# Sink scores in column tiles, an earlier weight row and a new order of loads in a windowed-attention and SwiGLU kernel

## The chip, the cores and the metric

The kernel runs on one core of a Trainium2 chip. Its time is the device time of one execution, in microseconds (us). The page and the trace come from one execution under the hardware profiler; its span runs from the first to the last instruction. The engines are called PE (TensorE), DVE (VectorE), ACT (ScalarE), POOL (GpSimd) and SP (SyncE). SP, ACT and POOL can also issue transfers, each on its own queue.

## The reference

Attention with a few sink keys and a sliding window, followed by a gated feed-forward network. There are 4 batches, 8 heads, 768 positions and a head size of 64; `n_sink` is 4 and `window` is 128.

```
scores = q @ k.T / sqrt(64)
keep   = (key < 4) or (0 <= query - key < 128)
a      = softmax(scores where keep)
x      = (a @ v), heads side by side: 3072 tokens x 512
xn     = x / sqrt(mean(x*x) + 1e-6) * rms_g
out    = (silu(xn @ w_gate) * (xn @ w_val)) @ w_out     # 512 -> 1536 -> 512
```

All inputs and the output are fp32; the kernel computes in bf16 with fp32 sums.

## The kernel before

**Blocks.** The 3072 tokens are 24 blocks `g` of 128 tokens, six in a batch `b` (`t` is the place in the batch). A query sees the keys of its own block and of the block before, so for each key block the kernel computes the scores of two query blocks at once (`nq = 2`; one in the last block of a batch). A query block that starts at position 256 or later (`t >= 2`) has its sink keys outside these two blocks, and they are handled apart.

**Steps of one block.** Loads of q, k and v go through the POOL queue, which casts fp32 to bf16. For the first blocks, a few loads (`F32_LOADS`) go through SP in fp32 and are cast by ACT or DVE (`cast`, L318). Blocks below `QK_DMA_FROM = 8` have q and k transposed on PE (`pe_t`, L415) and copied out of PSUM (`copy_t`, L422); the later ones are transposed by a DMA that SP issues (`dma_t`). Then come:
- `mask_bias` (L437), for blocks below `PE_MASKS`: a matmul of 512 columns writes -32768 where the mask forbids, into each of the four score banks, and the scores add to it.
- `scores` (L455): 8 matmuls of 64 rows, in pairs of row tiles. A block in `SPLIT` has its two query blocks scored apart.
- `exps` (L468) on ACT.
- For blocks that have no bias matmul: a mask that multiplies the exponentials on DVE (`mask_dve`, L485), or, from `POOL_MASK_FROM` on and for `t > 0`, selects on POOL (`mask_pool`, L490 and L495).
- `av` (L504, L514, L519) on PE, `normal` (L530, L531) and `rms` (L546 to L563) on DVE, `square` (L539) on ACT. `rms` multiplies by `gb`, the RMS weight row on all 128 partitions.
- The result x is transposed on PE (`pe_x`, L578) and copied (`copy_x`, L584), or, from block `X_DMA_FROM` on, by a DMA from SP (`dma_x`, L590).

**The weight row.** `grow` is one row of 512 fp32 numbers. `unit_gb` (L398) multiplies it with a column of ones on PE, which spreads it over the partitions, and `scale_gb` (L401) copies it out on ACT.

**Sinks.** `sink_k` (L594 to L598) puts the four sink keys of each head into a tile `ksk` that is zero elsewhere. `sink_s` (L621) computes the sink scores of two or four query blocks: four matmuls, one for each pair of heads, all adding into the same 128 rows of one PSUM bank; each has the 128 columns of `ksk` that begin at its pair's place, in which only that pair's 8 rows are not zero. `sink_e` (L629) takes the exponential, `sel` and `headm` bring the sink values of v into the matching rows (`sink_v`, L603; `sink_vm`, L612), and `av` adds one matmul with both.

**Feed-forward.** Four blocks make a group `G`. For each group the gate and value matmuls (L755) fill tiles of 128 x 512, cut into 4, 2 or 1 token chunks (`CHUNKS`). ACT takes tanh (L762), DVE makes `p` (L768) and `hT` (L778). `project` (L788) multiplies with `w_out`, ACT evacuates (L796) and SP stores.

**Order.** The order on every engine is worked out when the program is built, by the class `Plan`: each step has an estimated duration, its needs, a priority (smaller goes first) and the PSUM banks that it takes. The planner always places next the step that can start first, by its own clock; on a tie the smaller priority wins. Its model of transfers is `land`. The result is a fixed order: at run time each engine works in it and waits where data is missing. `LOADS` gives the order of loads on the POOL queue, `gate_of` holds a block's scores back until a given feed-forward step (`GATE_LEAD` steps earlier than its place), and `warm` puts up to `WARM` matmuls on zeros where PE would be idle.

Of the kernel before, what the change touches and what calls it, by code (L numbers as in the profile page):

```python
# [10 lines left out]
ACT = mybir.ActivationFunctionType  # L11
FP32 = mybir.dt.float32
BF16 = mybir.dt.bfloat16
I32 = mybir.dt.int32

P = 128
# [10 lines left out]
class Plan:  # L27
# [21 lines left out]
    def land(self, ring, first, work):  # L49


        r = self.rings
        if ring == "POOL":
            begin = max(first, r["POOL"], r["HW"])
            r["POOL"] = begin + (1.4 * work if begin < 8500 else work)
            self.loads -= 1
            return r["POOL"] + 520
        if ring == "HW":
            r["HW"] = max(first, r["HW"]) + work
            return r["HW"] + 900  # L60
        begin = max(first, r["TR"], r["POOL"])
        if self.loads:
            r["POOL"] = max(r["POOL"], first) + work
            work *= 2
        r["TR"] = begin + work
        return r["TR"] + (350 if ring == "TR" else 650)

    def run(self):
        free, users = dict(self.START), {}
        self.loads = sum(o["ring"] == "POOL" for o in self.ops)  # L70
        wait = {o["at"]: set(o["needs"]) for o in self.ops}
        cand = {e: [] for e in free}
        left = len(self.ops)
        for o in self.ops:
            for t in o["needs"]:
                users.setdefault(t, []).append(o)
            if not o["needs"]:
                for e in o["ways"]:
                    cand[e].append(o)
        busy, warm, mode, order = [], False, 0, []  # L80
        while left:
            first = None
            for e, found in cand.items():
                for o in found:
                    k = len(o["takes"])
                    if k > len(self.banks):
                        continue
                    ready = o["ready"] + self.HOP[e] if o["ready"] else 0
                    if k:
                        ready = max(ready, sorted(self.banks.values())[k - 1] + 40)  # L90
                    start = max(free[e], ready)
                    key = (start, o["prio"], ready, o["at"])
                    if first is None or key < first[0]:
                        first = key, e, o
            if first is None:
                raise RuntimeError("stuck: %s" % [
                    (o["gives"], list(wait[o["at"]])) for o in self.ops if o["at"] in wait
                ][:20])
            (start, *_), e, o = first
            for x in o["ways"]:  # L100
                cand[x].remove(o)
            wait.pop(o["at"])
            left -= 1
            ns, lat, fn = o["ways"][e]
            if e == "PE":
                busy = [(a, d) for a, d in busy if a > start - 3413]
                warm = start - free[e] < 4000 and (warm or sum(d for a, d in busy) > 3000)
                ns = ns if warm else 2 * ns
                if o["mode"] != mode:
                    ns, mode = ns + 110, o["mode"]  # L110
                busy.append((start, ns if mode < 2 else 0))
                lat = ns + 180
            for s in o["takes"]:
                i = min(self.banks, key=lambda i: (self.banks[i], i))
                del self.banks[i]
                self.held[s] = i
            free[e] = start + ns
            end = start + lat
            if o["ring"] is not None:
                end = self.land(o["ring"], end, o["work"]) + self.LATE  # L120
            for s in o["drops"]:
                self.banks[self.held[s]] = end + 12
            for t in o["gives"]:
                for x in users.pop(t, ()):
                    x["ready"] = max(x["ready"], end + 12)
                    w = wait[x["at"]]
                    w.discard(t)
                    if not w:
                        for way in x["ways"]:
                            cand[way].append(x)  # L130
            order.append((start, end, e, fn, o))
        return order
# [3 lines left out]
def kernel(  # L136
# [13 lines left out]
    nc = tc.nc  # L150

    B, H, S, D = q.shape
# [12 lines left out]
    GN = GB * P  # L165
    VW = D + 1
    HW = 4 * VW
    KSW = P + 2 * NS
    inv_sqrt_d = 1.0 / math.sqrt(D)
    F32_LOADS = ("qs0","ks0","qs1")  # L170
    GROW = "ACT"
    CAST_DVE = 1500
    MASKS_PRIO = -5
    POOL_AT = (0,1)
    DEPTH = 8
    LOADS = "k-1 v-0 qkv-2 w-0-2 v-1 qkv-3 w-2-4 w-4-6 w-6-8 w-8-9 w-9-12 qkv-4 wo-0-6 qkv-5 wo-6-12 qkv-8 qkv-6 qkv-7"
    LOADS += "".join(f" qkv-{g}" for g in range(9, NB))
    PE_MASKS = 4
    POOL_MASK_FROM = 14
    X_DMA_FROM = 8  # L180
    QK_DMA_FROM = 8
    LD = 16
    GATE_FROM = 6
    LOAD_LEAD = 9
    LEAD_FROM = 9
    WARM = 20
    GATE_LEAD = 10
    T_LEAD = 3
    SPLIT = (0,1,2)
    CHUNKS = (4,2,2)  # L190
    GB_PRIO = 2000

# [59 lines left out]
        dve(60, lambda b=b: nc.vector.memset(V16[b][:, :, :, D:VW], 1.0),  # L252
            gives=[("vone", b)], prio=-97 + b if b == 0 else -50)
    dve(150, lambda: nc.vector.memset(ones, 1.0), gives=["ones"], prio=-96)
    dve(70, lambda: nc.vector.memset(sel, 0.0), gives=["sel0"], prio=-39)
    if WARM:
        zeros = const.tile([P, P], BF16, name="zeros")
        dve(70, lambda: nc.vector.memset(zeros, 0.0), gives=["zeros"], prio=-99.6)
# [29 lines left out]

    def make_sel():
        nc.vector.tensor_copy(  # L290
            out=sel[:, 0:H * NS].rearrange("p (h s) -> p h s", s=NS),
            in_=ident[:, 0:NS].unsqueeze(1).to_broadcast((P, H, NS)),
        )
        nc.vector.reduce_sum(
            out=headm, in_=ident[:, 0:H * NS].rearrange("p (h s) -> p h s", s=NS),
            axis=mybir.AxisListType.X,
        )

# [2 lines left out]
    dve(130, other_bias, [("bias", 0)], [("bias", 1)], -60)  # L301
    dve(220, cut_ident, ["ident"], ["idnos"], -59)
    dve(700, make_masks, [("bias", 0), ("bias", 1)], ["masks"], MASKS_PRIO)
    dve(300, make_sel, ["ident", "sel0"], ["sel", "headm"], MASKS_PRIO + 1)

# [92 lines left out]
    def scale_gb():  # L400
        nc.scalar.mul(gb, BANK.pop(("gb",)), C3)  # L401

    pe(864, unit_gb, ["ones", "grow", ("s", 0, 0)], ["gbm"], GB_PRIO, takes=[("gb",)], mode=2)
    act(490, scale_gb, ["gbm", "table"], ["gb"], drops=[("gb",)])

    def qk_tile(b):
# [183 lines left out]
        nc.sync.dma_start_transpose(out=x_out(g), in_=T.pop(("xr", g)))  # L590

    def sink_k(b):
        ks = T["ksk", b] = sink.tile([P, HP * KSW], BF16, name="ksk")
        nc.vector.memset(ks, 0.0)  # L594
        ksv = ks.rearrange("p (h c) -> p h c", c=KSW)
        for hi in range(2):
            pr = slice(hi * D, (hi + 1) * D)
            nc.vector.tensor_copy(  # L598
                out=ksv[pr, :, hi * NS:(hi + 1) * NS], in_=T["qkT", b][pr, 1, :, 0:NS],
            )  # L600
# [17 lines left out]
    def sink_s(b, t, n):  # L618
        ps = bank(("ss", b, t))
        for hp in range(HP):  # L620
            nc.tensor.matmul(  # L621
                out=ps[:, 0:n * P], lhsT=T["ksk", b][:, hp * P:(hp + 1) * P],
                rhs=T["qkT", b][:, 0, hp, t * P:(t + n) * P],
                start=(hp == 0), stop=(hp == HP - 1),
            )

    def sink_e(b, t, n):
# [17 lines left out]
    for g in range(NB):  # L645
# [84 lines left out]
        if t == 0:  # L730
            dve(600, lambda b=b: sink_k(b),
                [("kT", g), ("s", g + 1)] + ([("ss", b - 2, i) for i in ((2, 4) if b - 2 < 2 else (2,))]
                               if b >= 2 else []), [("ksk", b)], 0.1 * g)
            for half in range(2):
                pe(115, lambda b=b, half=half: sink_v(b, half), [("v", g), ("vone", b), "sel", ("s", g)],
                   [("vs", b, half)], pa + 14, takes=[("vs", b, half)])
                dve(340, lambda b=b, half=half: sink_vm(b, half), [("vs", b, half), "headm"]
                    + ([("av", NT * (b - 2) + NT - 1, u) for u in range(2)] if b >= 2 else [])
                    + ([("vsk", b, 0)] if half else []),
                    [("vsk", b, half)], 0.1 * g, drops=[("vs", b, half)])  # L740
            for t0, n in ((2, 2), (4, 2)) if b < 2 else ((2, 4),):
                pe(4 * (n * 53 + 3), lambda b=b, t0=t0, n=n: sink_s(b, t0, n),
                   [("ksk", b), ("s", g + 1)] + [("qT", g + t0 + i) for i in range(n)],
                   [("ss", b, t0)], -1000.0 + 10 * (g + t0) + 2, takes=[("ss", b, t0)])
                act(n * 107 + 55, lambda b=b, t0=t0, n=n: sink_e(b, t0, n),
                    [("ss", b, t0), "table"] + ([("av", g - 1, u) for u in range(2)] if b else []),
                    [("esk", b, t0 + i) for i in range(n)], early, drops=[("ss", b, t0)])
# [169 lines left out]
```

The softmax here doesn't subtract the row's maximum and nothing guards it: scores larger than these inputs give would overflow.

## Time and profile before

| what | value |
|---|---|
| time, median of 3 runs | 249.78 us (248.58 to 250.07) |
| profiled run, its span | 249.03 us, 247.3 us |
| granted PE clock, mean of the span | 0.999 |
| DVE busy 60 to 66, 66 to 91, 91 to 103 us | 5.6 of 6, 24.1 of 25, 11.2 of 12 us |
| DVE busy 103 to 115, 115 to 132, 132 to 152 us | 11.1 of 12, 8.9 of 17, 18.8 of 20 us |
| first feed-forward matmul (L755) | 20.79 us |
| first matmul of feed-forward group 3 | 142.44 us |
| DMA queue of POOL, share of 16 engines | 76.3% |

Part 1 of the page gives the busy time of each engine. PE and PEld are matmuls and loads of their stationary operand. A group row reads: line, engine, operation, out<-in, shapes and count, then busy us and mean ns, then the idle time before it and what ended it. The chain of waits, in order of time, gives start and length in us of each piece that the end can be traced back through. DMA digits in the page are at 8 or 9 tenths for the first half of the span.

### The profile page before, as it was taken

What the parts mean: (1) busy time and instruction counts of PE and PEld (TensorE: products, weight loads), DVE (VectorE), ACT (ScalarE), POOL (GpSimd) and SP (SyncE); (2) the same over time, 40 slices, a digit from 0 to 9 for tenths busy, and PEclk for the clock granted to TensorE, in tenths of its full rate; (3) what the DMA queues carried; (4) which work ended last, traced back from release to release, by engine and by line L of the source; (5) the groups of instructions that cost most, each with busy time, mean ns of one, the idle gap of its engine ahead of it and who ended that gap; (6) DMA issues with size and microseconds to landing.
All of it is one profiled execution on the core that took longest, in us unless ns stands there. A gap on an engine that the chain in (4) does not pass through costs nothing.

```text
span 247.3 us, 5553 instructions
## 1 busy us (share of the span) xinstructions
PE 239.0 (97%) x2122; PEld 151.1 (61%) x2122; DVE 181.0 (73%) x477; ACT 129.5 (52%) x278; POOL 91.8 (37%) x121
## 2 busy tenths in 40 slices
PE   5899999999999999999999999999999999999994
PEld 2467998875788875587786544445555444444443
DVE  4278878798999999997377999998369980277700
ACT  3578366869655926662537466273556421333211
POOL 8976655759424756733703201230331000000000
PEclk9999999999999999999999999999999999999999
DMA  8999999999999999999990362201231002200022
GB/s 133 175 174 195 190 188 188 157 113 148 180 197 126 156 137 155 167 209 145 155 149 19 100 157 42 48 19 55 77 106 25 11 11 85 85 3 0 0 85 85
DMA packets 112523, 27.48 MB, mean 111 GB/s; under 512 B 102641, under 2 KB 109553, under 8 KB 112498
## 3 DMA queue, kind: packets, MB, share of 16 engines
q0 software_dynamic: 79664, 13.77, 76.3%
q1 hardware_dynamic: 32688, 13.25, 30.1%
q8 instruction: 16, 0.26, 0.4%
q10 hardware_dynamic: 146, 0.13, 0.2%
q14 instruction: 9, 0.07, 0.1%
HBM read 28.31 MB, written 6.29 MB: 140 GB/s over the span
## 4 chain that ended last, share of the span: by engine, by line
PE 84%; DVE 9%; DMA 3%; issue 2%; ACT 1%; POOLq 0%
PE v L755 23%; PE g L755 23%; PE o L788 22%; PE s L455 4%; DMA k<-in_k_dram 3%; PE av L519 2%; PE av L514 2%; PE ss L621 2%; DVE x L531 2%; DVE r L559 2%; DVE hT L778 1%; PE av L504 1%; PE o_last L806 1%; DVE p L768 1%; DVE xr L563 1%
## 5 line engine op out<-in xcount | busy, mean ns | idle before, releaser
L755 PE MATMUL v<-xnt,wv 128*128 128x128 bf16 (+2 forms) x528 | 70.9, 282 | 0.3 <-DVE hT L778 0.2
L762 ACT ACTIVATE th<-g 128x512 bf16<-128x512 f32 x72 | 43.0, 600 | 51.3 <-PE g L755 48.4
L755 PE MATMUL g<-xnt,wg 128*128 128x128 bf16 (+2 forms) x528 | 69.6, 282 | 0.2 <-DVE hT L778 0.2
L768 DVE SCALAR_TENSOR_TENSOR p<-th,g 128x512 bf16<-128x512 bf16 x72 | 48.4, 683 | 27.4 <-ACT th L762 27.2
L788 PE MATMUL o<-wo,hT 128*128 128x512 bf16 x276 | 65.3, 379 | 0.0
L755 PEld LDWEIGHTS <-wg 128*128 128x128 bf16 x528 | 43.6, 98 | 19.3 <-issue 0.3
L468 ACT ACTIVATE e<-s 128x512 bf16<-128x512 f32 (+1 forms) x108 | 49.2, 526 | 11.6 <-PE s L455 10.2
L755 PEld LDWEIGHTS <-wv 128*128 128x128 bf16 x528 | 43.2, 98 | 19.7 <-issue 1.2
L778 DVE TENSOR_TENSOR hT<-p,v 128x512 bf16<-128x512 bf16 x72 | 47.1, 681 | 2.9 <-PE v L755 2.2
L788 PEld LDWEIGHTS <-hT 128*128 128x128 bf16 x276 | 25.2, 98 | 27.0 <-issue 1.7
L490 POOL TENSOR_SCALAR_AFFINE_SELECT e<-e 128x512 bf16<-128x512 bf16 x18 | 11.6, 650 | 53.1 <-ACT e L468 42.8
L326 POOL DMA_DIRECT2D v<-in_v_dram x24 | 21.3, 889 | 14.7 <-DMA q<-in_q_dram 9.8
L322 POOL DMA_DIRECT2D k<-in_k_dram x23 | 20.4, 889 | 15.4 <-DMA v<-in_v_dram 8.5
L796 ACT ACTIVATE osb<-o 128x512 f32<-128x512 f32 x23 | 13.8, 601 | 19.5 <-PE o L788 19.5
L322 POOL DMA_DIRECT2D q<-in_q_dram x22 | 19.5, 886 | 11.1 <-DMA k<-in_k_dram 5.0
L539 ACT ACTIVATE sq<-x 128x512 bf16<-128x512 bf16 x24 | 15.2, 632 | 14.9 <-DVE x L531 14.8
L531 DVE TENSOR_TENSOR x<-av,rden 128x256 bf16<-128x256 f32 x48 | 20.4, 424 | 1.7
L563 DVE SCALAR_TENSOR_TENSOR xr<-x,r,gb 128x512 bf16<-128x512 bf16 x24 | 18.4, 765 | 0.9
L519 PE MATMUL av<-v,e 128*128 128x65 bf16 x192 | 17.0, 195 | 0.0
L514 PE MATMUL av<-v,e 128*128 128x65 bf16 x160 | 14.7, 193 | 0.2 <-ACT e L468 0.2
L455 PE MATMUL s<-qkT 64*128 64x256 bf16 (+1 forms) x216 | 14.9, 258 | 0.1
L485 DVE TENSOR_TENSOR e<-e,masks 128x1024 bf16<-128x1024 bf16 (+1 forms) x22 | 13.6, 635 | 1.4 <-ACT e L468 1.4
(72 smaller groups left out, 182.3 us busy)
## 6 DMA issues: line engine op xcount, KB each, us to landing
out_dram<-osb SPq DMA_DIRECT2D x23, 256.0 KB, 2.4
v<-in_v_dram POOLq DMA_DIRECT2D x24, 128.0 KB, 10.0
k<-in_k_dram POOLq DMA_DIRECT2D x23, 128.0 KB, 10.7
q<-in_q_dram POOLq DMA_DIRECT2D x22, 128.0 KB, 11.3
wo<-in_moe_w_out_dram POOLq DMA_DIRECT2D x2, 768.0 KB, 12.3
wg<-in_moe_w_gate_dram POOLq DMA_DIRECT2D x4, 256.0 KB, 8.0
wv<-in_moe_w_val_dram POOLq DMA_DIRECT2D x4, 256.0 KB, 8.3
stage<-in_q_dram SPq DMA_DIRECT2D x2, 256.0 KB, 4.7
```

Of the source, the lines that this page charges most:

```text
L322: nc.gpsimd.dma_start(out=T[name, g], in_=block_of(src, g))
L326: nc.gpsimd.dma_start(out=V16[b][:, t, :, 0:D], in_=block_of(v, g))
L455: nc.tensor.matmul(out=BANK[slot][:, j * 256 + n0 * P:j * 256 + n1 * P], lhsT=qkT[pr, 1, hp, t * P:(t + 1) * P], rhs=qkT[pr, 0, hp, (t + n ...
L468: nc.scalar.activation(out=T["e", g, u][:, 2 * hi:2 * hi + 2, n0:n1, :].rearrange("p x n c -> p x (n c)"), in_=ps.rearrange("p (j c) -> p ...
L519: nc.tensor.matmul(out=dest, lhsT=T["e", g, u][:, x, 0, :], rhs=V16[b][:, t, h, :], start=(t == 0), stop=True, skip_group_check=True,)
L531: nc.vector.tensor_tensor(out=T["x16", g][:, 4 * u:4 * u + 4, :], in0=pvv[:, :, 0:D], in1=rden.unsqueeze(2).to_broadcast((P, 4, D)), op=AL ...
L563: nc.vector.scalar_tensor_tensor(out=T["xr", g], in0=T.pop(("x16", g)).rearrange("p h d -> p (h d)"), scalar=r[:, 3:4], in1=gb, op0=ALU.mu ...
L755: nc.tensor.matmul(out=ps[:, i * n:(i + 1) * n], lhsT=w_sb[:, kt, ft * P:(ft + 1) * P], rhs=T["xnt", G][:, kt, cols], start=(kt == 0), sto ...
L762: nc.scalar.activation(out=T["th", key], in_=BANK[("g", key)], func=ACT.Tanh, scale=0.5,)
L768: nc.vector.scalar_tensor_tensor(out=T["p1", key], in0=T.pop(("th", key)), scalar=1.0, in1=BANK.pop(("g", key)), op0=ALU.add, op1=ALU.mult,)
L778: nc.vector.tensor_tensor(out=T[hk][:, i:i + n, cols], in0=T.pop(("p1", key)).rearrange("p (n c) -> p n c", n=n), in1=BANK.pop(("v", key)) ...
L788: nc.tensor.matmul(out=BANK[("o", G, tb)], lhsT=T["h", G, ft // 4][:, ft % 4, tb * P:(tb + 1) * P], rhs=wo[:, ft, :], start=(ft == 0), sto ...
```

## The change

1. **Sink scores.** The four matmuls of `sink_s` write four different sets of 32 PSUM rows (`tile_position=(0, hp * 32)`), each from 32 columns of a smaller `ksk`, instead of adding into one set of 128. `sel` and `headm` are laid out to match, and the memset of `sel` goes.
2. **Weight row.** `grow` is loaded by SP instead of ACT (`GROW`), and `unit_gb` no longer needs the first scores of block 0.
3. **Loads.** `F32_LOADS` are k and q of block 0, in that order; q of block 1 goes to the head of `LOADS`. The first weights and v of block 1 pass block 2's q, k and v; near the end blocks 8 and 6 change places.
4. **Where work is done.** `PE_MASKS` 4 to 2, `POOL_MASK_FROM` 14 to 16, `X_DMA_FROM` 8 to 9, `POOL_AT` (0,1) to (1,2) (the two selects that build the identity and the bias, among the loads on POOL), `CAST_DVE` 1500 to 600.
5. **Planner.** `WARM` 20 to 30, `GATE_LEAD` 10 to 6, `LEAD_FROM` 9 to 10, `SPLIT` without block 2; the model of an fp32 load that begins late, and of the modes that count as PE activity, changes.

```diff
-            r["HW"] = max(first, r["HW"]) + work
+            begin = max(first, r["HW"])
+            r["HW"] = begin + (1.25 * work if begin > 2500 else work)
...
-                busy.append((start, ns if mode < 2 else 0))
+                busy.append((start, ns if mode != 2 else 0))
...
-    KSW = P + 2 * NS
+    SW = P // HP
-    F32_LOADS = ("qs0","ks0","qs1")
-    GROW = "ACT"
-    CAST_DVE = 1500
+    F32_LOADS = ("ks0","qs0")
+    GROW = "SP"
+    CAST_DVE = 600
-    POOL_AT = (0,1)
+    POOL_AT = (1,2)
-    LOADS = "k-1 v-0 qkv-2 w-0-2 v-1 qkv-3 w-2-4 ... qkv-5 wo-6-12 qkv-8 qkv-6 qkv-7"
+    LOADS = "q-1 k-1 v-0 w-0-2 v-1 qkv-2 qkv-3 w-2-4 ... qkv-5 wo-6-12 qkv-6 qkv-8 qkv-7"
-    PE_MASKS = 4
-    POOL_MASK_FROM = 14
-    X_DMA_FROM = 8
+    PE_MASKS = 2
+    POOL_MASK_FROM = 16
+    X_DMA_FROM = 9
-    LEAD_FROM = 9
-    WARM = 20
-    GATE_LEAD = 10
+    LEAD_FROM = 10
+    WARM = 30
+    GATE_LEAD = 6
-    SPLIT = (0,1,2)
+    SPLIT = (0,1)
...
-    pe(864, unit_gb, ["ones", "grow", ("s", 0, 0)], ["gbm"], GB_PRIO, takes=[("gb",)], mode=2)
+    pe(1000, unit_gb, ["ones", "grow"], ["gbm"], GB_PRIO, takes=[("gb",)], mode=2)
...
-        ks = T["ksk", b] = sink.tile([P, HP * KSW], BF16, name="ksk")
+        ks = T["ksk", b] = sink.tile([P, HP * SW], BF16, name="ksk")
...
-                out=ps[:, 0:n * P], lhsT=T["ksk", b][:, hp * P:(hp + 1) * P],
+                out=ps[hp * SW:(hp + 1) * SW, 0:n * P],
+                lhsT=T["ksk", b][:, hp * SW:(hp + 1) * SW],
                 rhs=T["qkT", b][:, 0, hp, t * P:(t + n) * P],
-                start=(hp == 0), stop=(hp == HP - 1),
+                start=True, stop=True, tile_position=(0, hp * SW), skip_group_check=True,
...
-                pe(4 * (n * 53 + 3), lambda b=b, t0=t0, n=n: sink_s(b, t0, n),
+                pe(n * 53 + 16, lambda b=b, t0=t0, n=n: sink_s(b, t0, n),
...
-                   [("ss", b, t0)], -1000.0 + 10 * (g + t0) + 2, takes=[("ss", b, t0)])
+                   [("ss", b, t0)], -1000.0 + 10 * (g + t0) + 2, takes=[("ss", b, t0)], mode=3)
```

More of the change, by code (lines that the diff above doesn't have):

```diff
@@ L167 @@
     HW = 4 * VW
-    KSW = P + 2 * NS
+    SW = P // HP
     inv_sqrt_d = 1.0 / math.sqrt(D)
-    F32_LOADS = ("qs0","ks0","qs1")
-    GROW = "ACT"
-    CAST_DVE = 1500
+    F32_LOADS = ("ks0","qs0")
+    GROW = "SP"
+    CAST_DVE = 600
     MASKS_PRIO = -5
-    POOL_AT = (0,1)
+    POOL_AT = (1,2)
     DEPTH = 8
-    LOADS = "k-1 v-0 qkv-2 w-0-2 v-1 qkv-3 w-2-4 w-4-6 w-6-8 w-8-9 w-9-12 qkv-4 wo-0-6 qkv-5 wo-6-12 qkv-8 qkv-6 qkv-7"
+    LOADS = "q-1 k-1 v-0 w-0-2 v-1 qkv-2 qkv-3 w-2-4 w-4-6 w-6-8 w-8-9 w-9-12 qkv-4 wo-0-6 qkv-5 wo-6-12 qkv-6 qkv-8 qkv-7"
     LOADS += "".join(f" qkv-{g}" for g in range(9, NB))
-    PE_MASKS = 4
-    POOL_MASK_FROM = 14
-    X_DMA_FROM = 8
+    PE_MASKS = 2
+    POOL_MASK_FROM = 16
+    X_DMA_FROM = 9
     QK_DMA_FROM = 8
@@ L254 @@
     dve(150, lambda: nc.vector.memset(ones, 1.0), gives=["ones"], prio=-96)
-    dve(70, lambda: nc.vector.memset(sel, 0.0), gives=["sel0"], prio=-39)
     if WARM:
@@ L290, in make_sel @@
         nc.vector.tensor_copy(
-            out=sel[:, 0:H * NS].rearrange("p (h s) -> p h s", s=NS),
-            in_=ident[:, 0:NS].unsqueeze(1).to_broadcast((P, H, NS)),
+            out=sel.rearrange("p (a s) -> p a s", s=NS),
+            in_=ident[:, 0:NS].unsqueeze(1).to_broadcast((P, P // NS, NS)),
         )
         nc.vector.reduce_sum(
-            out=headm, in_=ident[:, 0:H * NS].rearrange("p (h s) -> p h s", s=NS),
+            out=headm.rearrange("p (x i) -> p x i", i=2),
+            in_=ident.rearrange("p (x i s) -> p x i s", x=HP, s=NS)[:, :, 0:2, :],
             axis=mybir.AxisListType.X,
@@ L303 @@
     dve(700, make_masks, [("bias", 0), ("bias", 1)], ["masks"], MASKS_PRIO)
-    dve(300, make_sel, ["ident", "sel0"], ["sel", "headm"], MASKS_PRIO + 1)
+    dve(300, make_sel, ["ident"], ["sel", "headm"], MASKS_PRIO + 1)
     def block_of(src, g):
@@ L592, in sink_k @@
     def sink_k(b):
-        ks = T["ksk", b] = sink.tile([P, HP * KSW], BF16, name="ksk")
+        ks = T["ksk", b] = sink.tile([P, HP * SW], BF16, name="ksk")
         nc.vector.memset(ks, 0.0)
-        ksv = ks.rearrange("p (h c) -> p h c", c=KSW)
+        ksv = ks.rearrange("p (h c) -> p h c", c=SW)
         for hi in range(2):
```

## The prediction, made before the change was run

> **What bounds the kernel now.** I read the page's busy shares first, then the waits of TensorE (PE) after the start, then the chain that ended last, then the groups by shape.
>
> The page's first part:
>
> ```profile
> PE 239.0 (97%) x2122; PEld 151.1 (61%) x2122; DVE 181.0 (73%) x477; ACT 129.5 (52%) x278; POOL 91.8 (37%) x121
> ```
>
> A busy PE is not proof of a bound, since matmul records overlap. The waits of PE alone between 20 and 244 us are the proof:
>
> ```profile
> PE ss L621 <- DVE qkT L422: 0.3, 1, 0.3
> PE v L755 <- DVE hT L778: 0.2, 1, 0.2
> PE g L755 <- DVE hT L778: 0.2, 1, 0.2
> ```
>
> After 20 us PE lacks work for 0.7 us in total. So the span is the time until PE is fed without gaps (about 20.5 us) plus a dense stream, and only two things move it: an earlier dense stream, or less in the stream (or a new hole in it). The start is a different stage; the chain in order of time (start, us, what):
>
> ```profile
> 1.32 6.58 DMA k<-in_k_dram
> 7.94 0.61 PE k L415 x4
> ...
> 8.76 0.54 PE s L455 x8
> ...
> 9.95 2.00 PE gb L398 x2
> 11.95 0.54 PE s L455 x8
> 12.49 0.56 PE av L519 x8
> ...
> 13.80 0.43 PE q L415 x4
> 14.23 0.43 PE k L415 x4
> ...
> 17.47 0.33 PE x L578 x4
> ```
>
> The fp32 spread of the weight row (gb) sits between the first and second scores, for 2.00 us, and everything below queues behind it. Four transposes take 0.43 us at 14.23 and 0.33 at 17.47: PE is at half clock until about 14.7 us. The groups by shape (busy us, mean ns):
>
> ```profile
> L437 PE MATMUL s<-bias,ident 128*128 128x512 bf16 x12 | 3.1, 382 | 0.0
> L621 PE MATMUL ss<-qkT,ksk 128*128 128x256 bf16 x16 | 2.4, 273 | 0.3 <-DVE qkT L422 0.3
> L621 PE MATMUL ss<-qkT,ksk 128*128 128x512 bf16 x8 | 2.1, 379 | 0.0
> L485 DVE TENSOR_TENSOR e<-e,masks 128x1024 bf16<-128x1024 bf16 x18 | 12.1, 684 | 1.4 <-ACT e L468 1.4
> ```
>
> These means hold latency that the next matmul hides; the chain gives the pace: four matmuls of 512 columns take 0.86 us, four of 256 take 0.43 to 0.44, four transposes 0.23 in a dense stretch.
>
> **What the Trainium skill says.** (1) "TensorEngine Tiling (Array Packing)", Key Properties: tiles run independently, but changing the tiling mode drains the array. Before has one change of mode to compare: after eight 64-row score matmuls the next matmul starts about 0.1 us late (129.97 start, 0.43 us of streaming in pairs, next at 130.52). (2) "TensorE: Matmul & The Clock Gate", Measured speedup vs the span model: three column tiles gave 2.38 times, not 3. No run here shows column tiles yet. (3) The tiling page, Restrictions: column tiles lose the fast weight load; with 24 weight loads of 32 columns I put that at nothing. (4) The clock page: PE idles at half clock and is released by activity; the trace agrees, with its four bias matmuls of 583 to 631 ns at 3.9 us and 379 to 420 ns from 14.7 us on.
>
> **The change, part by part.**
>
> *Sink scores.* Six groups of four matmuls: four groups of 256 columns, two of 512. In the stream they cost 4 x 0.43 + 2 x 0.86 = 3.4 us; the first (19.93) lies in the start, so 3.0 us lie in the dense stream. If four tiles give about 3 times (estimate from the clock page's 2.38 for three), 1.0 us is left. Each group brings one or two changes of mode at about 0.1 us: 5 x 0.14 = 0.7. Net -1.3 us. Bounds: -1.8 (perfect overlap, one change each), +0.9 (no overlap at all, two changes). The smaller ksk (memset of 272 words, 285 ns, becomes 64 words) frees under 0.2 us of DVE, four times: off the path.
>
> *Bias matmuls of blocks 2 and 3.* Eight matmuls leave, 0.86 us each block. Block 3's set (22.71 us) is in the dense stream: -0.9. Block 2's (16.61) is in the start and counted there. In return DVE multiplies four tiles more, 4 x 684 ns = 2.7 us. Block 2's lie near 20 us, block 3's near 37 us, where DVE is busy 6.7 of 10 and 21.2 of 25 us; PE waited for DVE only 0.7 us in all, so 0. Bounds 0 to +0.7 (one mask of latency on a hidden tile's chain).
>
> *Weight row.* grow's issue goes from ACT (0.53 us) to SP, between the two fp32 loads; qs0 is then issued at about 1.85, where the second load stood at 1.33, so its landing (5.7) slips to about 6.2. gb no longer waits for the first scores, so its 2.0 us at half clock come before them. PE has idle time there (4.0 of the first 10 us, in the table of stretches), but make_bias now stands behind the second load on the POOL queue (POOL_AT), 0.9 us later, so bias matmuls start at about 4.75 instead of 3.87. PE needs, at half clock, 1.86 (bias) + 2.0 (gb) + 4 x 0.43 to 0.63 (transposes) before both scores of block 0: first scores at 9.2 to 10 instead of 8.76, second at 9.8 to 10.6 instead of 11.95. Net -1.3 to -2.1 on the chain to av and x.
>
> *Loads.* q of block 1 goes from the SP queue (fp32, 256 KB) to the head of the POOL queue. Behind it on that queue wait all others, one issue (0.89 us) later each; w-0-2 and v-1 pass qkv-2. In the order of landing, the first feed-forward tile needs w-2-4: it landed at 18.8 (wg) and 20.2 (wv), used at 20.79 and 23.58. One HWDGE load less (third landing 2.4 us after the second, with k-1 in between) against one software load more (0.85 us each at steady pace): w-2-4 the same or up to 0.6 earlier. So PE can't be dense before about 18.5: the start gains at most 2.3 us. I take -1.6 (with block 2's bias matmuls gone from it); bounds -0.5 to -2.3.
>
> *Later weights.* wg of columns 6 to 8 landed at 24.18 and is used at 26.80; wg 9 to 12 at 28.94, used at 31.3; k-4 at 32.6, used at 35.7. That is 2.3 to 3 us of room, just enough for a PE that is 1.6 + 0.9 us ahead.
>
> *Other moves.* Block 8's x is transposed on PE (+0.23 us, and a copy of 0.42 on DVE or 0.6 on ACT) and leaves SP's queue (issue 1.19 us, 6.8 us to landing): +0.3, and the DMA transposes behind it come a little earlier. Masks of blocks 14 and 15 go from POOL (8 of 32 selects, 0.64 us each) to DVE, 4 x 684 ns; DVE is busy only 8.9 of 17 us from 115 to 132: 0. WARM fillers, ten more of 0.107 us at half clock, lie in gaps of the start; SPLIT loses block 2 and costs its second scores a wait for q-3 (landed 16.0, used at 19): 0.
>
> Sum: -1.6 - 0.9 - 1.3 + 0.3 = -3.5 us of the 247.3 us span: 243.8. The profiled run took 249.03, the other runs shown 248.58 to 250.07; -1.4% of the median is **246.3 us**.
>
> **The rivals.**
>
> *Half gain.* The start stays bound by weights and by half-clock PE (-0.5), or the column tiles do not overlap (+0.9 for -1.3). For it: the room before w-2-4 is thin, and no trace shows the overlap. The first alone gives -2.4 us (247.4), the second -1.3 (248.5), both -0.2 (249.6).
>
> *Slower: feed-forward group 3 starves.* Its first matmul starts at 142.44, and the last x it needs lands at 141.8 (DVE row xr at 139 us and its DMA transpose): 0.6 us of room. GATE_LEAD 6 instead of 10 makes block 15's scores wait for the seventh tile of group 2 (end at 122.2) where they ran at 118.06: 4.1 us. If blocks 14 and 15 carry this to their x, PE has used up group 2's projections and stands still: +4.1 less the last sink's 0.5, span 250.9, time 253.4. Against it: block 15's tiles lie ready from 123 us on and are used only after 131, so 8 us of delay are needed before this decides, and a PE that is 3 us ahead uses up 3 of them.
>
> *All the gain there is.* Start at -2.3 and sinks at -1.8 give -4.7 us, 245.0. More fillers may also release the clock before 14.7 us; for: PE has more to do early; against: the weights at 18.5 us cap what the start can give. Below 244.5 something is needed that I don't see.
>
> **How the numbers follow.** A run-to-run spread of 0.6% makes about 1% the least that can be told from no change. My forecast, from all its gain to the edge of half gain (244.5 to 247.2), 0.52; better than that 0.10; half gain (247.3 to 250.2) 0.25; starved, above 250.2, 0.13. Faster by over 1% (below 247.3): 0.63; slower by over 1% (above 252.3): 0.10; between: 0.27. The range 243.8 to 250.6 leaves out about 0.07 below and 0.12 above.
>
> **What would show it.** gb ahead of the first scores, and second scores at 10 to 11 us; first g tile at 18.5 to 19.3; L437 with 8 matmuls; each 512-column sink group ending under 0.5 us from its start to the next matmul; PE's waits after 20 us still under 1.5 us; group 3's first g at about 139. The forecast is wrong if sink matmuls start 0.2 us apart, if the first g tile stays at 20.5 or later, or if PE waits several us for hT, xnt or a weight load.

## The result, and the profile after

The changed kernel takes 246.64 us (median of four runs, 245.98 to 246.97), the kernel before 249.75 us (four runs, 248.58 to 250.07). The ratio is 0.9881, with a 95% interval of 0.9841 to 0.992: 1.2% faster, where 246.3 us was forecast. The span of the profiled run went from 247.3 to 244.3 us. Line numbers are one to two higher in the changed kernel: scores L456, bias matmuls L438, weight row L399, sinks L622, feed-forward L757.

First the busy shares of the page, and then the waits of PE between 20 and 241 us (what PE waited for: us in total, times, longest).

```profile
PE 232.6 (95%) x2098; PEld 147.8 (61%) x2120; DVE 183.7 (75%) x482; ACT 131.2 (54%) x276; POOL 88.8 (36%) x114
```

```profile
PE o L790 <- issue: 0.6, 4, 0.2
PE g L757 <- DVE rden L531: 0.3, 1, 0.3
PE g L757 <- DMA wg<-in_moe_w_gate_dram: 0.2, 1, 0.2
```

PE is still the bound: 1.1 us of waits after 20 us (0.7 before). Busy PE fell by 6.4 us, but not all of that is gain: 22 matmul records are missing in this trace (2098 against 2120 weight loads), and a matmul's record holds latency (a second run of the changed kernel, with all 2120 records, has 235.9 us busy). The groups by shape:

```profile
L486 DVE TENSOR_TENSOR e<-e,masks 128x1024 bf16<-128x1024 bf16 x26 | 17.5, 686 | 0.9 <-ACT e L469 0.8
...
L622 PE MATMUL ss<-qkT,ksk 128*32 128x256 bf16 x16 | 1.2, 283 | 0.0
L399 PE MATMUL gb<-grow,ones 1*128 1x512 f32 x2 | 1.1, 640 | 0.0
L438 PE MATMUL s<-bias,ident 128*128 128x512 bf16 x4 | 1.0, 378 | 0.0
L622 PE MATMUL ss<-qkT,ksk 128*32 128x512 bf16 x8 | 0.8, 390 | 0.0
```

Eight bias matmuls with `ident` are gone, DVE has eight more masks of 686 ns, and the sink groups are busy for 2.0 us in place of 4.5. A mean of 390 ns for one 512-column sink matmul looks unchanged (379 before); only the timeline shows that four now run together. The timeline of PE (start, length, what) before, and then after:

```profile
165.04 1.03 PE L621 MATMUL ss<-qkT,ksk 128*128 128x512 bf16 x4
165.91 1.03 PE L755 MATMUL v<-xnt,wv 128*128 128x512 bf16 x4
```

```profile
171.62 0.40 PE L622 MATMUL ss<-qkT,ksk 128*32 128x512 bf16 x4
171.96 0.61 PE L456 MATMUL s<-qkT 64*128 64x256 bf16 x8
```

From the first sink matmul to the next other matmul: 0.87 us before, 0.34 us after. A group of 256 columns took 0.44 and takes 0.22 us.

The start of the profiled run, PE alone (a bracket is idle time and what ended it):

```profile
8.46 0.40 PE L456 MATMUL s<-qkT 64*128 64x128 bf16 x8
8.79 1.12 PE L399 MATMUL gb<-grow,ones 1*128 1x512 f32 x2
9.84 0.47 PE L456 MATMUL s<-qkT 64*128 64x128 bf16 x8
...
18.14 0.61 PE L757 MATMUL g<-xnt,wg 128*128 128x128 bf16 x8
19.75 0.62 PE L757 MATMUL g<-xnt,wg 128*128 128x128 bf16 x8 [1.00 <-DMA wg<-in_moe_w_gate_dram]
```

Two things are to be seen. The weight row still lies **between** the first and the second scores. And it took 1.12 us where it took 2.07 before, because PE was at full clock from about 8.4 us in this run. The same kernel in another run (from the last experiments) was at half clock until about 14.2 us, as the kernel before was (14.7), so that one is the fair comparison:

```profile
8.76 0.61 PE L456 MATMUL s<-qkT 64*128 64x128 bf16 x8
9.30 2.07 PE L399 MATMUL gb<-grow,ones 1*128 1x512 f32 x2
11.30 0.61 PE L456 MATMUL s<-qkT 64*128 64x128 bf16 x8
...
16.20 0.39 PE L579 MATMUL x<-ident,xr 128*128 128x128 bf16 x4
...
19.86 1.06 PE L757 MATMUL g<-xnt,wg 128*128 128x128 bf16 x16
```

| start of, us | before | after | after, other run |
|---|---|---|---|
| second scores of block 0 | 11.88 | 9.84 | 11.30 |
| x of block 0 on PE | 17.40 | 14.47 | 16.20 |
| first feed-forward matmul | 20.79 | 18.14 | 19.86 |
| first matmul of group 3 | 142.44 | 138.92 | 139.36 |
| end of the span | 247.3 | 244.3 | 244.7 |

Between the two profiles with a like clock the first feed-forward matmul comes 0.9 us earlier, and the end 2.6 us. The 0.9 us is not firm. Runs 1, 4, 11 and 12 below have the same order on PE up to this matmul, and their clock was released at 15.4 to 16.9 us: it starts at 20.38 to 20.72 us in them. Run 2, with the order of the kernel before and a release at 16.1 us, has it at 20.74. The two lines are from run 12 and run 2:

```profile
20.72 1.06 PE L757 MATMUL g<-xnt,wg 128*128 128x128 bf16 x16
20.74 1.07 PE L757 MATMUL g<-xnt,wg 128*128 128x128 bf16 x16
```

So with a late clock this point moved by 0 to 0.9 us, and the spans of runs 4, 11 and 12 are 244.9 to 245.2 us all the same: most of the gain comes behind it. The profiled run, whose clock was released 6 us sooner, ends only 0.4 us before the other: of its lead of 1.7 us at the first feed-forward matmul, 1.00 us went into the wait for wg.

**What left the stream** can be counted. In dense stretches 512 columns take 0.215 us, so a matmul streams 2.4 columns per ns. Over all matmuls of the two runs that have every record (the scores, in pairs of row tiles, count half, and the sinks in column tiles a quarter), that is 221.0 us before and 217.5 us after: eight bias matmuls -1.71, sinks -2.56 (3.41 to 0.85), four more transposes +0.21, ten more fillers +0.53. The end came only 2.6 us earlier, so the rest (idle time, half clock, changes of tiling mode) grew by 0.9 us, from 26.3 to 27.2. The changes of mode that the column tiles bring are about 0.8 us of it, as runs 1 and 2 show.

### The profile page after: what moved, and what is told of

It is laid out like the page before. It is cut to its first block, busy times and chain, and to the rows that moved or that the text cites. A ratio compares the mean times of both kernels' runs of the same rounds, so it can differ in the third digit from the quotient of the medians.

```text
span 244.3 us, 5510 instructions
## 1 busy us (share of the span) xinstructions
PE 232.6 (95%) x2098; PEld 147.8 (61%) x2120; DVE 183.7 (75%) x482; ACT 131.2 (54%) x276; POOL 88.8 (36%) x114
## 4 chain that ended last, share of the span: by engine, by line
PE 77%; DVE 9%; POOL 5%; DMA 4%; issue 3%; ACT 0%; POOLq 0%; DVEq 0%; ACTq 0%
PE o L790 23%; PE g L757 21%; PE v L757 21%; PE s L456 4%; DMA wg<-in_moe_w_gate_dram 4%; DVE hT L780 2%; PE av L520 2%; DVE p L770 2%; PE av L515 2%; DVE r L560 2%; POOL v L327 1%; DVE xr L564 1%; PE av L505 1%; PE o_last L808 1%; DVE x L532 1%
## 5 line engine op out<-in xcount | busy, mean ns | idle before, releaser
L757 PE MATMUL g<-xnt,wg 128*128 128x128 bf16 (+2 forms) x525 | 69.8, 282 | 1.6 <-DMA wg<-in_moe_w_gate_dram 1.2
L757 PE MATMUL v<-xnt,wv 128*128 128x128 bf16 (+2 forms) x522 | 71.0, 281 | 0.3
L790 PE MATMUL o<-wo,hT 128*128 128x512 bf16 x263 | 62.6, 379 | 1.2 <-issue 0.6
L757 PEld LDWEIGHTS <-wg 128*128 128x128 bf16 x528 | 43.1, 98 | 21.0 <-DMA wg<-in_moe_w_gate_dram 1.5
L757 PEld LDWEIGHTS <-wv 128*128 128x128 bf16 x528 | 42.6, 98 | 18.5 <-issue 0.8
L469 ACT ACTIVATE e<-s 128x512 bf16<-128x512 f32 (+1 forms) x104 | 48.4, 542 | 6.6 <-PE s L456 6.3
L491 POOL TENSOR_SCALAR_AFFINE_SELECT e<-e 128x512 bf16<-128x512 bf16 x14 | 9.4, 680 | 61.8 <-ACT e L469 48.8
L323 POOL DMA_DIRECT2D k<-in_k_dram x23 | 20.5, 890 | 15.9 <-DMA v<-in_v_dram 7.0
L323 POOL DMA_DIRECT2D q<-in_q_dram x23 | 20.5, 893 | 13.0 <-DMA k<-in_k_dram 3.8
L531 DVE RECIPROCAL rden<-av 128x4 f32<-128x4 f32 x48 | 8.5, 177 | 15.4 <-PE av L520 15.3
L486 DVE TENSOR_TENSOR e<-e,masks 128x1024 bf16<-128x1024 bf16 (+1 forms) x30 | 18.9, 650 | 1.0 <-ACT e L469 0.8
L564 DVE SCALAR_TENSOR_TENSOR xr<-x,r,gb 128x512 bf16<-128x512 bf16 x24 | 19.0, 790 | 0.9
L520 PE MATMUL av<-v,e 128*128 128x65 bf16 x192 | 16.9, 194 | 0.0
```

The costliest lines, as they stand in the source:

```text
L323: nc.gpsimd.dma_start(out=T[name, g], in_=block_of(src, g))
L469: nc.scalar.activation(out=T["e", g, u][:, 2 * hi:2 * hi + 2, n0:n1, :].rearrange("p x n c -> p x (n c)"), in_=ps.rearrange("p (j c) -> p ...
L520: nc.tensor.matmul(out=dest, lhsT=T["e", g, u][:, x, 0, :], rhs=V16[b][:, t, h, :], start=(t == 0), stop=True, skip_group_check=True,)
L564: nc.vector.scalar_tensor_tensor(out=T["xr", g], in0=T.pop(("x16", g)).rearrange("p h d -> p (h d)"), scalar=r[:, 3:4], in1=gb, op0=ALU.mu ...
L757: nc.tensor.matmul(out=ps[:, i * n:(i + 1) * n], lhsT=w_sb[:, kt, ft * P:(ft + 1) * P], rhs=T["xnt", G][:, kt, cols], start=(kt == 0), sto ...
L790: nc.tensor.matmul(out=BANK[("o", G, tb)], lhsT=T["h", G, ft // 4][:, ft % 4, tb * P:(tb + 1) * P], rhs=wo[:, ft, :], start=(ft == 0), sto ...
```

## The experiments

All ratios are against the kernel before, run on the same chip. On PE, runs 1, 2 and 12 keep the planned order, and run 8 only adds fillers to it. In the others the planner orders the steps anew, so such a run shows its edit together with the order that comes of it. `WARM`, `LEAD_FROM`, `SPLIT` and the two changes of the planner's model were not undone by themselves. The changed kernel, run again with the last four, is the base for what undoes a part of it; the third column is the difference of the two ratios:

> The changed kernel once more, as the common base of this group of runs. If the early release of the PE clock in its first profile (8.4 us) was chance, this profile may show it at 14 us or later, with the first feed-forward tile at 20.4 us instead of 18.1 and a span of about 245.2; the ratio to the kernel before stays at 0.988.

No edit. Measured: 246.95 us, ratio 0.9901 [0.9882, 0.992].

| run | ratio [95%] | against the base, or before |
|---|---|---|
| 1 changed, sinks without tiles | 0.9976 [0.9963, 0.9989] | +0.75%, 1.9 us lost |
| 2 before, sinks in tiles | 0.9943 [0.9924, 0.9962] | 1.4 us gained on before |
| 3 changed, weight row as before | 0.9925 [0.9897, 0.9954] | +0.24%, overlap |
| 4 changed, GATE_LEAD 10 | 0.9907 [0.9881, 0.9932] | none |
| 5 before, weight row as changed | 1.0078 [1.0046, 1.011] | 1.9 us lost on before |
| 6 changed, w-2-4 ahead of block 3 | 0.9995 [0.9982, 1.0007] | +0.94%, 2.3 us lost |
| 7 changed, PE_MASKS 4 | 0.9969 [0.9957, 0.998] | +0.68%, 1.7 us lost |
| 8 changed, denser fillers | 0.9874 [0.9846, 0.9903] | -0.27%, overlap |
| 10 changed, whole old start | 0.9967 [0.9952, 0.9982] | +0.66%, 1.6 us lost |
| 11 changed, X_DMA_FROM 8 | 0.9901 [0.9882, 0.992] | none |
| 12 changed, POOL_MASK_FROM 14 | 0.9921 [0.9901, 0.9941] | +0.20%, overlap |

**1 and 2: the column tiles alone.** Run 1 takes the old form of the sinks into the changed kernel, run 2 the new form into the kernel before, each with the layout of `ksk`, `sel` and `headm` that belongs to it; the order on PE stays. The edit of run 1, in part:

```diff
-                out=ps[hp * SW:(hp + 1) * SW, 0:n * P],
-                lhsT=T["ksk", b][:, hp * SW:(hp + 1) * SW],
+                out=ps[:, 0:n * P], lhsT=T["ksk", b][:, hp * P:(hp + 1) * P],
...
-                start=True, stop=True, tile_position=(0, hp * SW), skip_group_check=True,
+                start=(hp == 0), stop=(hp == HP - 1),
```

> The changed kernel with the old sink scores (four matmuls that add into one set of 128 rows) in the same order of work. Theory A, that the dense PE stream bounds the kernel and the tiles shorten it: the three sink groups of 256 columns that lie in the stream go from 0.22 to 0.44 us and the two of 512 from 0.33 to 0.86, so the span rises by 3 x 0.21 + 2 x 0.5 = 1.6 us against the changed kernel, to about 245.9. Theory B, that the gain comes from the new order of work and the tiles only shift PE time into waits for weights and x: span within 0.4 us of the changed kernel's 244.3.

> The kernel before with the column tiles alone, its planned order unchanged. Theory A: span 247.3 - 1.6 = 245.7, because all but the first group lie in a stream that waits for nothing. Theory B, that group 3 of the feed-forward starts on its last x with 0.6 us of room and so swallows what is saved ahead of it: only the last sink group (0.5 us) counts, span 246.8.

Measured: 248.68 and 247.71 us. By the ratios the tiles are worth 1.4 us on the kernel before and 1.9 us on the changed one. The timeline of PE in run 2, and in run 1:

```profile
163.79 1.03 PE L757 MATMUL v<-xnt,wv 128*128 128x512 bf16 x4
164.75 0.40 PE L622 MATMUL ss<-qkT,ksk 128*32 128x512 bf16 x4
165.08 1.04 PE L757 MATMUL v<-xnt,wv 128*128 128x512 bf16 x4
```

```profile
173.62 1.03 PE L622 MATMUL ss<-qkT,ksk 128*128 128x512 bf16 x4
174.57 0.61 PE L456 MATMUL s<-qkT 64*128 64x256 bf16 x8
```

In run 2 the group occupies 0.33 us, of which 0.215 is streaming: leaving the mode costs about 0.1 us. The last v matmul before it started at 164.44, so entering costs 0.309 - 0.216 = 0.09 us. Not every group pays both. Four of the six lie beside score matmuls, which are in row tiles, a mode of their own, and there the old form paid for one change too: in run 1 the scores follow 0.95 us after the first sink matmul, where streaming takes 0.86. From the start of the matmul before a group to the start of the one after it, the six groups together are 1.76 us shorter in the changed kernel than in run 1, and 1.7 to 1.8 us shorter in run 2 than before. That is the 2.56 us of streaming less about 0.8 for changes of mode, and both ratios agree with it within their intervals.

**3 and 5: the weight row alone**, undone in the changed kernel (3), put into the kernel before (5). The edit of run 3:

```diff
-    GROW = "SP"
+    GROW = "ACT"
...
-    pe(1000, unit_gb, ["ones", "grow"], ["gbm"], GB_PRIO, takes=[("gb",)], mode=2)
+    pe(864, unit_gb, ["ones", "grow", ("s", 0, 0)], ["gbm"], GB_PRIO, takes=[("gb",)], mode=2)
```

> The changed kernel with the weight row loaded from ACT and spread after the first scores again, as before; the planner orders the rest anew. Theory A, that the start is bound by the landing of the second pair of weight columns (19.7 us in the changed kernel): the first feed-forward tile still ends at about 20 us and the span moves by less than 0.5 us. Theory B, that the early weight row is what shortened the start and released the PE clock early (8.4 us against 14.7): the clock is released 3 us later or more, the first tile ends after 21 us, and the span rises by 1 us or more.

> The kernel before with the weight row alone moved: loaded from SP, spread without waiting for the first scores. The prediction's step says that this alone shortens the start by about 1.6 us: second scores at 10 to 10.6 us instead of 11.9, first feed-forward tile at 19.2, span about 245.7. If instead the start is set by the landing of the weights and by the clock of PE, the second scores come earlier but the first tile stays at 20 to 21 us and the span within 0.5 us of 247.3.

Measured: 247.55 and 251.27 us. Run 5 is the only kernel here in which gb does go ahead of the first scores, and it is 0.8% slower, which neither branch of the expectation had. PE in run 5:

```profile
7.84 1.03 PE L415 MATMUL k<-ident,k 128*128 128x128 bf16 x8 [1.68 <-DMA k<-in_k_dram]
8.81 2.07 PE L398 MATMUL gb<-grow,ones 1*128 1x512 f32 x2
10.81 0.61 PE L455 MATMUL s<-qkT 64*128 64x128 bf16 x8
...
12.53 0.61 PE L455 MATMUL s<-qkT 64*128 64x128 bf16 x8
...
24.58 1.61 PE L755 MATMUL g<-xnt,wg 128*128 128x128 bf16 x26
```

grow's issue stands on SP ahead of the second fp32 load, which is k's here: ACT's cast of k began at 7.03 us (5.76 before), PE's two sets of k transposes ran together at 7.84, and by then there was no idle time left in front of the first scores for gb to fill. The second scores start at 12.53 instead of 11.88, and the first feed-forward matmul at 24.58 instead of 20.79. In the changed kernel k is loaded first, and q of block 1 comes early. Run 3 is 0.24% from the base with overlapping intervals: that the weight row's own two lines gain or lose anything in the changed kernel is not shown.

**10: the whole start as before**, with tiles, masks and the rest as changed: `F32_LOADS`, `GROW`, `POOL_AT`, `CAST_DVE`, `LOADS` and the `unit_gb` line.

```diff
-    F32_LOADS = ("ks0","qs0")
-    GROW = "SP"
-    CAST_DVE = 600
-    POOL_AT = (1,2)
+    F32_LOADS = ("qs0","ks0","qs1")
+    GROW = "ACT"
+    CAST_DVE = 1500
+    POOL_AT = (0,1)
...
```

> The changed kernel with the whole start as before: three fp32 loads, the weight row from ACT and behind the first scores, the old order of loads, of the two selects on POOL and the old cast price. If the start is worth what the prediction took (1.6 us), the time rises by 1.6 us against the changed kernel. If the gain lies in the PE stream (tiles and bias matmuls, 2.1 to 3.2 us by the runs so far) and the start is held by the landing of the loads in either form, it rises by less than 0.6 us.

Measured: 248.38 us, 1.4 us more than the base's median (1.6 by ratio). The waits of PE from 12 to 60 us in run 10:

```profile
PE q L416 <- DMA q<-in_q_dram: 1.2, 1, 1.2
PE x L579 <- DVE xr L564: 0.7, 1, 0.7
PE k L416 <- DMA k<-in_k_dram: 0.5, 2, 0.3
PE g L757 <- DMA wg<-in_moe_w_gate_dram: 0.5, 1, 0.5
```

and in the changed kernel, run again:

```profile
PE s L456 <- ACT qkT L423: 0.6, 1, 0.6
PE x L579 <- DVE xr L564: 0.4, 1, 0.4
PE av L520 <- ACT e L469: 0.3, 1, 0.3
```

With the old start PE waits 3.4 us there (two smaller waits of 0.3 and 0.2 not shown), with the new one 1.3 us. This is one profile of each, and run 10's had full clock sooner (from 6.5 us, half again from 10.0 to 13.4), which brings PE to its loads sooner: the profile of the changed kernel that was released at 8.4 us waits 2.4 us in the same stretch. From 20 to 26 us the difference is clearer: run 10 waits 1.5 us there (for x, wg and wv), the two profiles of the changed kernel 0.2 and 0.4. Run 10's first feed-forward matmul came at 18.39 us, earlier than 19.86, and it still ended 1.2 us later. So, as far as these profiles show, the new start's worth lies mainly in keeping the shorter stream fed. Two ratios point the same way: tiles alone on the kernel before give 0.9943, while tiles, fewer bias matmuls and the rest on the old start give 0.9967 (the intervals overlap slightly). Which of its six settings does it was not separated, and the new start on the kernel before was not run: both are open.

**7: bias matmuls back for blocks 2 and 3.**

```diff
-    PE_MASKS = 2
+    PE_MASKS = 4
```

> The changed kernel with bias matmuls for blocks 0 to 3 again, and four mask multiplications fewer on DVE. If the eight matmuls of 512 columns cost what they take in the stream, block 3's set at least: span up by 0.9 us (both sets: 1.7), to 245.2 or more. If PE has idle time there while weights land, up by less than 0.4 us.

Measured: 248.46 us, 1.7 us lost. The group of run 7:

```profile
L438 PE MATMUL s<-bias,ident 128*128 128x512 bf16 x12 | 4.0, 464 | 0.0
```

Eight more matmuls at 0.213 us of streaming are 1.71 us. The span of run 7, 246.6 us, less its 219.2 us of streaming leaves 27.4 us, against 27.2 in the changed kernel. So both sets count in full, block 2's too.

**6: the first weights earlier.** The load of the second pair of weight columns goes ahead of block 3's q, k and v.

```diff
-    LOADS = "q-1 k-1 v-0 w-0-2 v-1 qkv-2 qkv-3 w-2-4 w-4-6 ... qkv-6 qkv-8 qkv-7"
+    LOADS = "q-1 k-1 v-0 w-0-2 v-1 qkv-2 w-2-4 qkv-3 w-4-6 ... qkv-6 qkv-8 qkv-7"
```

> The changed kernel with w-2-4 loaded ahead of block 3's q, k and v. If the landing of w-2-4 (19.7 us) alone holds up the dense PE stream, the first tile ends 1.5 us or more earlier and the span falls by 1 us. If the later weights, which land when they did, and block 3's scores take its place as what PE waits for, the first tile is earlier but the span moves by less than 0.5 us.

Measured: 248.99 us, 2.3 us lost, which neither branch of the expectation had, though the first feed-forward matmul starts at 18.05 (19.86 in the base run at a like clock). The waits of PE from 12 to 35 us:

```profile
PE x L579 <- DVE xr L564: 1.9, 2, 1.3
```

The weights' landing is not the only bound: PE now waits for x instead, and giving the weights a place takes it from block 3's loads.

**8: the clock.** Three filler matmuls for one in the first eight fillers, and eight behind k's first transposes.

```diff
-        nc.tensor.matmul(out=ps[:, 0:P], lhsT=zeros, rhs=zeros, start=True, stop=True)
+        for _ in range(3 if i < 8 else 1):
+            nc.tensor.matmul(out=ps[:, 0:P], lhsT=zeros, rhs=zeros, start=True, stop=True)
...
+        if (n, g) == ("k", 0):
+            for _ in range(8):
+                nc.tensor.matmul(out=BANK[("warm",)][:, 0:P], lhsT=zeros, rhs=zeros, start=True, stop=True)
```

> The changed kernel with more matmuls on zeros in the two gaps of PE in the first 7 us (24 instead of 8 at the start, and 8 more behind the first transposes); nothing else moves. The profiles so far show the clock of PE released at 7.8 to 8.4 us in two runs and at 14.7 to 16.6 us in four. If idle PE at 2 to 4 and 6 to 7 us is why the release is missed in most runs, it is now at 9 us or earlier each time, and the median falls to that of the best runs, about 246.0 (0.5 us or more below the changed kernel's 246.6). [...]if fillers only delay the bias matmuls, it rises.

Measured: 246.26 us, the lowest median of all, but its interval overlaps the base's; it is not shown to be better. Its stretches (us, PE busy, PEld, DVE, ACT, POOL, granted clock, DMA, GB/s):

```profile
15.00:20.00 5.00, 3.41 (x49) 2.15 (x43) 3.04 (x15) 3.50 (x11) 3.28 (x5) 0.84 1.75 184
20.00:26.00 6.00, 6.00 (x100) 5.97 (x98) 4.93 (x11) 3.84 (x9) 3.90 (x6) 0.85 1.53 193
```

The clock was released at 4.8 us, and lost again from 18.4 to 21.9 us after PE had waited for block 3's k (1.3 us) and q (0.9 us). Early release brought the work forward to the loads, and there it waited. About 1 us of the wait for k is this run's own: k landed at 17.96 us, and at 16.57 to 16.93 in the profiles with the same loads.

**4, 11 and 12: settings charged with little or nothing.**

```diff
-    GATE_LEAD = 6
+    GATE_LEAD = 10
```

> The changed kernel with GATE_LEAD 10 as before. The rival of the prediction said that 6 holds back blocks 14 and 15 and starves feed-forward group 3. If so, 10 is faster: group 3's first g comes earlier than 138.9 us without a wait and the span falls by 1 us or more. If the gate only decides which of several ready steps comes first (my theory), the span stays within 0.6 us of 244.3.

```diff
-    X_DMA_FROM = 9
+    X_DMA_FROM = 8
```

> The changed kernel with X_DMA_FROM 8: block 8's x goes back from PE to a DMA transpose. The prediction charged the move to PE with 0.23 us of stream. If that is all, this version is 0.2 to 0.3 us faster than the changed kernel; if the DMA transposes behind it come later and feed-forward group 2 or 3 starts later, it is slower by up to 1 us. It is also the candidate for a version that beats both.

```diff
-    POOL_MASK_FROM = 16
+    POOL_MASK_FROM = 14
```

> The changed kernel with the masks of blocks 14 and 15 on POOL again, four multiplications of 0.68 us fewer on DVE. The prediction put them at nothing, because DVE has room from 115 to 132 us: within 0.4 us of the changed kernel. If DVE is a second bound there, it is 1 us or more faster.

Measured: 246.78, 246.86 and 247.41 us. The first two cannot be told from the base, the third only by 0.2% with overlap. How near group 3 is to an edge is seen at its first matmul, in run 3, in run 11, and in the changed kernel:

```profile
138.94 1.02 PE L757 MATMUL g<-xnt,wg 128*128 128x512 bf16 x4 [1.28 <-DVE r L560]
```

```profile
139.50 1.02 PE L757 MATMUL g<-xnt,wg 128*128 128x512 bf16 x4 [0.37 <-DVE r L560]
```

```profile
138.92 1.02 PE L757 MATMUL g<-xnt,wg 128*128 128x512 bf16 x4 [0.34 <-DVE rden L531]
```

DVE from 115 to 132 us in the changed kernel has room left with the masks of blocks 14 and 15 on it, 14.67 of 17 us (8.9 before):

```profile
115.00:132.00 17.00, 16.68 (x163) 12.25 (x163) 14.67 (x38) 10.02 (x20) 1.34 (x2) 1.00 1.09 98
```

## Why the prediction was right, and where its steps were not

The forecast of 246.3 us is 0.3 us from the measured 246.64, and the view of what bounds the kernel held: PE stays dense after 20 us, and most of what leaves its stream leaves the time. But the sum came out by terms that do not all stand, and in part by luck.

- **Sinks, forecast -1.3: -1.4 and -1.9 by the ratios (runs 2 and 1), -1.54 by the starts on PE for the five groups that the forecast counted.** Right in sign; the term that was mis-sized is the overlap. It is 4 times, not 3: in one group of the changed kernel the four start at 66.133, 66.136, 66.140 and 66.143 us, and the five groups keep 0.75 us of streaming, not 1.0. The Trainium skill, "TensorE: Matmul & The Clock Gate", section Measured speedup vs the span model, states a lag of about 4 ns between tiles, and the 3.3 ns here agree; its 2.38 times for three tiles is less than these groups reach inside a stream. Changes of mode were put at 0.7 us for five groups, and they cost that: 2.24 us of streaming went, and 1.54 were gained. The weight loads of the tiles, put at nothing, took 92 ns each for 32 columns, where 128 columns took 98 before. "TensorEngine Tiling (Array Packing)", Key Properties, states that a change of mode drains the array, and no price; here a change takes about 0.1 us.
- **Bias matmuls, forecast -0.9 for block 3 and block 2's hidden in the start: -1.7 for both (run 7).** The failed term is block 2's: it was put into the start, which was taken to be bound by weights at 18.5 us, but it counts in full. DVE's extra masks at 0: right (runs 7 and 12, and PE's waits).
- **Weight row, forecast -1.3 to -2.1 on the chain: the mechanism failed.** The step that said gb comes before the first scores, because its need for them was gone, is wrong. Its priority of 2000 stayed. By the planner's own clock gb is ready from 4.0 us on, but each time PE comes free another step with a smaller number is ready too, or no PSUM bank is free, so gb still follows the first scores; with -2000 in its place the plan puts it ahead (that kernel was not run). Where gb does go ahead (run 5, in whose plan PE has nothing else ready at that moment), the kernel is slower. The prediction did see grow's issue push the second fp32 load back on SP (5.7 to 6.2 us forecast; ACT's cast of q began at 6.33), but not that in that gap PE then has nothing to work on. The second scores are at 11.30 us where they were at 11.88, 0.6 us and not 1.3 to 2.1, and even that is not shown to be the edit's: in run 2, with the order of the kernel before and a clock released at 16.1 us, they are at 11.13, because k landed 0.8 us sooner.
- **The start as a whole, forecast -1.6: 1.4 to 1.6 us when it is undone (run 10).** The size agrees for another reason: less waiting behind the start, as run 10's waits show. With a late clock the first feed-forward matmul came at 19.86 us and, in runs 1, 4, 11 and 12, at 20.38 to 20.72, not at the 18.5 to 19.3 forecast; two of the five are past the 20.5 us that the prediction named as a sign of being wrong. The profiled run's 18.14 was ahead of it, with an early clock, and then stood still for 1.00 us.
- **Loads.** That PE could not be dense before the second pair of weight columns lands held in the profiled run (wg at 19.71 us, 18.83 before). In the other run and in runs 1, 4, 11 and 12 it landed at 18.45 to 18.64, "the same or up to 0.6 earlier" as forecast, but there PE reached its first feed-forward matmul 1.4 to 2.2 us after that: with a late clock the work planned ahead of it on PE, and not this landing, set the start. Nor is the landing the sole bound where it comes early (run 6). The later weights' 2.3 to 3 us of room were enough: 0.2 us of waits for wg after 20 us.
- **Block 8's x on PE, forecast +0.3: not seen (run 11).** The 0.21 us of streaming that run 11 saves does not show in its time; in its profile PE waits 0.37 us at group 3, where the base's profile has no wait.
- **Rivals.** Starvation of group 3 did not come: 0.34 us of waiting there, and GATE_LEAD 10 changes nothing that can be told from the base (run 4). Half gain by tiles that do not overlap is out. Its other form, a start that gains only 0.5 us, fits the first feed-forward matmul with a late clock; what the kernel gained beyond that came from the stream and from behind the start. A clock released earlier was part of the third rival; it happened in the profiled run, at 8.4 us, and was worth little.

The parts do not add up. Undone one by one, tiles (1.9), bias matmuls (1.7) and the start (1.4 to 1.6) lose 5.0 to 5.2 us; together they gain 2.5 to 3.1. The prediction summed them as if each were on its own; it came out near because its terms together were some 1.6 us too small (3.5, where the single undoings give 5.1), which covers most of the 2 to 2.6 us that the interaction takes. Two errors cancelled, and that is luck. Run 10's waits show a part of the interaction; the rest stays open.

## What to carry to other kernels

Where one engine runs a dense stream, count the streaming time that an edit takes out, and then ask whether the stage that feeds it can follow: a shorter stream behind an unchanged start turns part of its gain into waits. Four small matmuls of one moving size and 32 columns each overlapped fully in column tiles here, so their price was that of one matmul and up to two changes of mode; beside work that is in another mode already, one of the changes is not new. When an order is planned by the program, removing a dependency need not move the step; its priority and the arrival of its other inputs have to be followed through the plan.

## What the runs showed of the hardware beside this

- **The PE clock is released at different times in the same kernel:** 8.4 us in one profiled run, 14.2 us in another; over all kernels here 4.8 to 17 us. It can be lost again while PE is busy part of the time: half clock came back for 3.4 us in run 8, after PE had been busy 1.8 of the 3.4 us before, and for 3.4 us in run 10, after 2.7 of 3.4. Between the two profiles of the changed kernel a release 6 us earlier moved the end by 0.4 us.
- **One pause in the loads.** In most profiled runs one landing of the POOL queue came about 1 us late, at a place that differs between runs of the same kernel: wg at 19.71 us, 2.2 us after the v before it (0.8 in the other run), and in the other run the next wg at 22.1 us, 2.3 us after the wv before it (1.3 in the first). Its cause stays open.
